# A fused scan and MLP kernel: block 0's preparation reordered, the first two scans put above the next block's preparation, and block 0's MLP input loaded from ScalarE's queue

## The chip, the cores and the metric

The kernel runs on one core of a Trainium2 chip. The metric is device time in microseconds (us), the median of three runs. Each core has a matrix engine (TensorE, PE in the profile), a vector engine (VectorE, DVE), an activation engine (ScalarE, ACT), GpSimd (POOL) and SyncE (SP), which in this kernel issues most of the DMAs. Each engine works through its own instructions strictly in the order in which the compiler wrote them, DMA issues included.

## The reference, cut to what matters

```python
# attention: 4 batches, 8 heads, 768 steps, head size 40
for t in range(S):
    y[:, :, t] = einsum('bhd,bhde->bhe', rt, state)
    Sa = einsum('bhde,bhe->bhd', state, at)
    state = state * wt - einsum('bhd,bhe->bhde', Sa, bt) + einsum('bhd,bhe->bhde', vt, kt)
x = y as (4*768, 320)
# MLP1, 320 -> 2048 -> 320
h = x @ w_in; g = maximum(h, 0) + alpha * minimum(h, 0); x = g @ w_out
# MLP2, 320 -> 1536 -> 320
g = x @ w_gate; out = (g * sigmoid(g) * (x @ w_val)) @ w_out
```

All arrays are fp32, except that weights reach the kernel as 64-bit words and are converted on the chip.

## The kernel before

The 768 time steps are cut into six blocks of 128. A block has four items, one for each batch; an item is one batch with 8 heads and 128 steps, and a scan goes through it in two chunks of 64 steps. Items are numbered 0 to 23, so items 0 to 3 are block 0.

**Preparation** (`prep_a`, `prep_b`, one pair for each item). ScalarE copies the decay into `wseg` (L540), VectorE scans it (L545, L552) and multiplies (`AN` L559 and `kbt`). TensorE makes `mnp` (L584) and the transposes `kbp` (L612). ScalarE takes the results out of PSUM: into `tt` (L590, L593), into `AN` (L597, which GpSimd then masks in L598) and into `KB` (L615). Four items fill one `tt`.

**Inverse** (`inverse(m)`, one for each block). It inverts the small triangular systems in `tt`: a VectorE transpose out of `tt` (L630), 31 steps on VectorE (L645, L653), two transposes (L656, L658), then TensorE's `eps` (L666) and `dps` (L685) with ScalarE copies between them. The second `eps` in the program is that of `inverse(1)`; no scan of block 1 can use its `tt` before that.

**Scan** (`seq(i, ch)`). One chunk runs around four engines: `zp` on TensorE (L749), `zs` on ScalarE (L751), `pp` on TensorE (L759), `ut` and `pv` on ScalarE (L761, L763), transposes on TensorE (L767, L771), `gs` and `s` on ScalarE (L773, L778), `gp` on TensorE (L782), a masked copy on VectorE, `yp` on TensorE (L797, L801), and the new state and `pv` on VectorE (L805, L809). After its second chunk a scan stores its output to `xd` in DRAM from ScalarE's queue (L817). The scan that comes next on the same side (`ch` is 0 or 1) begins with ScalarE's copy into `pv` (L717).

**MLP1** (`mlp1(j)`, one for each block). `fill_x` loads `xd[j]` into `xa` (L299, L303, four DMAs for a fill) and splits it into `xh`, `xl` (L218, L219) and `xst` (L304, L305). A step is 8 matmuls `u` (L274), the PReLU `g` (L314 on ScalarE, L315 on VectorE), the split into `gh` and `gl`, and 8 matmuls `d` (L280 to L286) of the step before. `mlp1(0)` is special: its first 8 steps run on the half of the columns that batches 0 and 1 give (256 wide), the next 8 on the other half, and only the rest on all 512. So the first half needs only scans 0 and 1.

**Weights** are converted in the first part of the program by all engines (`raw` to `wz`, `wy`, `wc`, `wd`).

MLP1 of the last blocks and all of MLP2 come after the last scan; MLP2 takes the last third of the time.

**What sets the order.** The generators above are interleaved by `drive(...)`, and each piece is given a priority by lowering or raising `tc.cur_priority`; a scheduler then writes out one order for each engine, a piece with a lower number first where its inputs allow. `lifted(n)` lowers the number by n inside it. Scans 0 and 1 run with `SP = 3000`, the preparation of block 1 (`rest1`, ending with `inverse(1)`) with `HP2 = 3000`, the fill of `mlp1` with `XPRI = 1000`.

Of the kernel before, what the change touches and what calls it, by code (L numbers as in the profile page):

```python
# [18 lines left out]
XPRI = 1000  # L19
# [44 lines left out]
L = 64  # L64
HALF = 32
LOOK = 2
TRB = 5
LATE = 20
XLEAD = 6
# [4 lines left out]
def kernel(  # L74
# [63 lines left out]
    def ago(n):  # L138
        return ups[-n] if len(ups) >= n else None
# [151 lines left out]
        xst = pool.tile([128, n], F32R, tag="xst", name="xst")  # L291
        return xh, xl, xst

    def fill_x(pool, xs, src, c0, c1):
        xh, xl, xst = (x[..., c0:c1] for x in xs)
        for j in range(3):
            xa = pool.tile([128, c1 - c0], F32, tag="xa", name="xa", bufs=XAB[0])
            if j < 2:
                nc.sync.dma_start(out=xa, in_=src[j * 128:j * 128 + 128])  # L299
                split(xa, xh[:, j], xl[:, j], nc.vector)  # L300
            else:
                for p in (lo, hi):
                    nc.sync.dma_start(out=xa[p], in_=src[256:DM])  # L303
                nc.scalar.copy(out=xst, in_=xa)  # L304
                nc.vector.tensor_tensor(out=xst[hi], in0=xa[hi], in1=xst[hi].bitcast(F32), op=ALU.subtract)  # L305

# [31 lines left out]
    def mlp1(j, early=0):  # L338
# [15 lines left out]
        seen = set()  # L354
        for f, c0, c1 in plan:
            if not seen & {(c0, c1), (0, half) if early and c0 == 0 else (c0, c1)}:
                with lifted(), held_by(ago(XLEAD) if j == NM - 1 else None):
                    b0, b1 = c0 // TB, c1 // TB
                    fill_x(xp1, xs, xd[j][:, b0:b1].rearrange("f b t -> f (b t)"), c0, c1)
                seen.add((c0, c1))  # L360
                yield
            t = fetch(wp1, 2 * f, True, j, done)
            ps = e1p["psu"].tile([128, c1 - c0], F32, tag="u", name="u")
            done.append(up_mm(ps, t, tuple(x[..., c0:c1] for x in xs)))
            yield
            if len(pend) == (2 if j == NM - 1 else DEP):
                down(*pend.pop(0))
            pend.append((f, c0, c1, *prelu(e1p["gp3"] if j == NM - 1 and fs.index(f) % 3 == 2 else gp1, ps, f, c1 - c0)))
            yield
# [196 lines left out]
    def prep_b(i):  # L566
# [14 lines left out]
        for g in range(2):  # L581
# [9 lines left out]
            for h, q in ((0, 1), (1, 3)):  # L591
                pr = slice(32 * q, 32 * q + 32)
                nc.scalar.copy(out=mc[pr, gsl, 0:HALF], in_=ps[pr, :, h, HALF:L])  # L593
            for h, pr in ((0, hi), (1, lo)):
                am = an[pr, h, g * SH:g * SH + SH]
                if AMK & (1 if i < B else 2 if i < 2 * B else 4):
# [5 lines left out]
                else:  # L602
                    mark["prep"] = nc.vector.tensor_tensor(
                        out=am, in0=ps[pr, :, h, :], in1=mask[pr].unsqueeze(1).to_broadcast([64, SH, L]), op=ALU.mult,
                    )
            yield
        kb = it["KB"] = (item_x if i < XI else item_q).tile([128, NSEG * 2 * D + 64 - D], F32, tag="KB", name="KB")
        nc.gpsimd.memset(kb[:, NSEG * 2 * D:], 0.0)
        for g in range(NSEG // 4):
            ps = bank([128, 4, 2, 64], "kbp", i)  # L610
            for j in range(4):
                nc.tensor.transpose(  # L612
                    ps[:, j].rearrange("p h e -> p (h e)"), kbt[:, 4 * g + j].rearrange("p j t -> p (j t)"), ident
                )
            nc.scalar.copy(  # L615
                out=kb[:, 8 * g * D:8 * (g + 1) * D].rearrange("p (s h e) -> p s h e", h=2, e=D), in_=ps[:, :, :, 0:D]
            )
            yield

    def scr(m, j):  # L620
# [269 lines left out]
        )  # L890
    else:
        drive(
            (seq(0, 0), N_SEQ, SP), (seq(1, 1), N_SEQ, SP),
            (take(rest1, int(nrest * RA)) if RA < 1 else rest1, FAC * nrest, HP2),
            (take(c1, NC1), NC1 - EC - EC0, CP),
        )
# [217 lines left out]
```

## Time and profile before

| what | value |
|---|---|
| median of three runs | 1230.73 us (1230.57, 1230.73, 1231.91) |
| profiled execution | 1229.82 us, its span 1228.1 us, granted clock 0.944 |
| PE busy | 1095.4 us, 89% of the span |
| DVE busy | 759.5 us, 62% |
| ACT busy | 602.0 us, 49% |
| POOL busy | 287.4 us, 23% |

The profiled execution is 0.91 us shorter than the median, and 1.7 us of it lie outside its span. Shares are means over stages that have different limits: the first 95 us hold the preparation and inverse of block 0, 95 to 220 us the first four scans with the preparation and inverse of block 1, 220 to 705 us the other scans beside MLP1, and what follows has no scan.

### The profile page before, as it was taken

What the parts mean: (1) busy time and instruction counts of PE and PEld (TensorE: products, weight loads), DVE (VectorE), ACT (ScalarE), POOL (GpSimd) and SP (SyncE); (2) the same over time, 40 slices, a digit from 0 to 9 for tenths busy, and PEclk for the clock granted to TensorE, in tenths of its full rate; (3) what the DMA queues carried; (4) which work ended last, traced back from release to release, by engine and by line L of the source; (5) the groups of instructions that cost most, each with busy time, mean ns of one, the idle gap of its engine ahead of it and who ended that gap; (6) DMA issues with size and microseconds to landing.
All of it is one profiled execution on the core that took longest, in us unless ns stands there. A gap on an engine that the chain in (4) does not pass through costs nothing. (4 is left out here: it accounts for less than half of the span.)

```text
span 1228.1 us, 24433 instructions
## 1 busy us (share of the span) xinstructions
PE 1095.4 (89%) x9056; PEld 934.2 (76%) x9056; DVE 759.5 (62%) x1624; ACT 602.0 (49%) x1495; POOL 287.4 (23%) x452
## 2 busy tenths in 40 slices
PE   4146687999999898899989999999999999999998
PEld 4145577877878787788777787787788888888887
DVE  7798988598589669949865434879522323223222
ACT  5559568655954665675655433545332323222222
POOL 8335433401212230341354000536300000000000
PEclk9669776988999998999999999999999999999999
DMA  5534688565554534645486464795010101010000
GB/s 146 186 133 147 214 271 288 172 193 171 158 156 135 175 114 145 194 153 154 125 280 210 148 206 138 250 353 164 1 48 1 48 1 48 1 37 13 22 1 22
DMA packets 94885, 166.36 MB, mean 135 GB/s; under 512 B 13232, under 2 KB 43184, under 8 KB 94768
## 3 DMA queue, kind: packets, MB, share of 16 engines
q1 hardware_dynamic: 86608, 160.88, 41.2%
q10 hardware_dynamic: 8160, 3.93, 1.1%
q8 instruction: 72, 1.18, 0.4%
q14 instruction: 45, 0.37, 0.1%
HBM read 136.98 MB, written 27.79 MB: 134 GB/s over the span
## 5 line engine op out<-in xcount | busy, mean ns | idle before, releaser
L218 ACT CAST gh<-g 128x512 fp32r<-128x512 f32 (+1 forms) x176 | 105.5, 600 | 162.8 <-DVE g L1050 116.2
L1050 DVE TENSOR_TENSOR g<-pv,sg 128x512 f32<-128x512 f32 x72 | 49.7, 691 | 206.3 <-PE pv L274 201.3
L219 DVE TENSOR_TENSOR gl<-g,gh 128x512 fp32r<-128x512 f32 (+1 forms) x176 | 121.9, 692 | 85.7 <-ACT gh L218 83.0
L274 PE MATMUL u<-xh,wt 128*128 128x512 f32 (+1 forms) x416 | 149.0, 401 | 13.5 <-DVE g L315 11.2
L315 DVE SCALAR_TENSOR_TENSOR g<-g,neg,u 128x512 f32<-128x512 f32 (+1 forms) x104 | 73.0, 703 | 88.9 <-ACT g L314 88.4
L274 PEld LDWEIGHTS u<-xh,wt 128*128 128x128 f32 x416 | 80.1, 196 | 32.7 <-DVE g L315 14.4
L314 ACT ACTIVATE g<-u 128x512 f32<-128x512 f32 (+1 forms) x104 | 58.6, 564 | 90.4 <-PE u L274 86.1
L274 PE MATMUL pg<-xh,w 128*128 128x512 f32 x288 | 102.6, 394 | 0.3 <-ACT sg L1048 0.3
L1048 ACT ACTIVATE sg<-pg 128x512 f32<-128x512 f32 x72 | 43.0, 598 | 120.6 <-PE pg L274 120.6
L274 PE MATMUL pv<-xh,w 128*128 128x512 f32 x288 | 100.5, 390 | 0.0
L1034 PE MATMUL o<-w,gh 128*128 128x320 f32 x288 | 87.5, 310 | 2.6 <-ACT gh L218 2.6
L1035 PE MATMUL o<-w,gh 128*128 128x320 f32 x288 | 87.8, 309 | 0.0
L281 PE MATMUL d<-gl,wt 128*128 128x512 f32 (+1 forms) x208 | 82.3, 398 | 1.2 <-DVE gl L219 1.2
L740 POOL COPY gs<-raw_v 64x160 f32<-64x160 f32 x96 | 40.8, 425 | 177.3 <-PE yp L797 108.6
L274 PE MATMUL u<-xl,wt 128*128 128x512 f32 (+1 forms) x208 | 80.8, 389 | 0.0
L653 DVE TENSOR_TENSOR la<-la,tmp 128x96 f32<-128x96 f32 (+43 forms) x306 | 79.3, 285 | 2.0
L282 PE MATMUL d<-gh,wt 128*128 128x512 f32 (+1 forms) x208 | 80.1, 387 | 0.0
L645 DVE TENSOR_TENSOR tmp<-la 128x96 f32<-128x96 f32 (+43 forms) x306 | 78.1, 279 | 1.8
L584 PE MATMUL mnp<-AN,kbt 128*128 128x128 f32 x384 | 59.6, 305 | 21.6 <-DVE AN L559 15.2
L598 POOL TENSOR_SCALAR_AFFINE_SELECT AN<-AN 64x256 f32<-64x256 f32 x96 | 52.2, 544 | 111.2 <-ACT AN L597 99.0
L1036 PE MATMUL o<-w,gl 128*128 128x320 f32 x288 | 77.2, 311 | 1.0 <-DVE gl L219 0.9
L280 PE MATMUL d<-gh,wt 128*128 128x512 f32 (+1 forms) x208 | 72.6, 402 | 2.8 <-DMA wt<-wd 2.8
(123 smaller groups left out, 2635.3 us busy)
## 6 DMA issues: line engine op xcount, KB each, us to landing
wt<-wd SPq DMA_DIRECT2D x98, 384.0 KB
wt<-wd SPq DMA_DIRECT2D x98, 320.0 KB
wd<-wc SPq DMA_DIRECT2D x24, 384.0 KB
raw<-in_moe_w_out_dram SPq DMA_DIRECT2D x28, 320.0 KB
raw_bk<-in_bk_dram SPq DMA_DIRECT2D x48, 160.0 KB
wd<-wc SPq DMA_DIRECT2D x20, 320.0 KB
raw<-in_moe_w_in_dram SPq DMA_DIRECT2D x16, 256.0 KB
raw_v<-in_v_dram SPq DMA_DIRECT2D x24, 160.0 KB
```

What stands on the lines that cost most here:

```text
L218: nc.scalar.copy(out=h, in_=raw)
L219: eng.tensor_tensor(out=l, in0=raw, in1=h.bitcast(F32), op=ALU.subtract)
L274: last = nc.tensor.matmul(ps, lt, rh, start=(i == 0), stop=(i == len(ops) - 1))
L280: nc.tensor.matmul(ps, wh, gh, start=first, stop=False)
L281: nc.tensor.matmul(ps, wh, gl, start=False, stop=False)
L282: nc.tensor.matmul(ps, wl, gh, start=False, stop=last)
L315: nc.vector.scalar_tensor_tensor(g, g, neg[:, f:f + 1], ps, ALU.mult, ALU.add)
L645: nc.vector.tensor_tensor(out=tv, in0=ml[:, kk + 1:HALF, kk:kk + 1].to_broadcast([128, nr, ns]), in1=tl[:, kk:kk + 1, c0:c0 + ns].to_broad ...
L653: mark["inv"] = nc.vector.tensor_tensor(out=dst, in0=dst, in1=tv, op=ALU.subtract)
L1034: nc.tensor.matmul(ops[q], gh[:, ts], wh, start=first, stop=False)
L1035: nc.tensor.matmul(ops[q], gh[:, ts], wl, start=False, stop=False)
L1036: nc.tensor.matmul(ops[q], gl[:, ts], wh, start=False, stop=last)
```

## The change

It has three parts.

1. `LATER = 800`: for the items of block 0, the copies into `AN` with their mask, and the whole `KB` part, get a number that is higher by 800, so that the `tt` copies of later groups may be put ahead of them.
2. `FIRST = 6000`: scans 0 and 1 run with 6000 in place of 3000, above the preparation of block 1.
3. The fill of `mlp1(0)` (both halves) is lifted by 6000 in place of 1000, and its `xa` DMAs are issued by ScalarE in place of SyncE.

```diff
-    def fill_x(pool, xs, src, c0, c1):
+    def fill_x(pool, xs, src, c0, c1, eng=nc.sync):
...
-                nc.sync.dma_start(out=xa, in_=src[j * 128:j * 128 + 128])
+                eng.dma_start(out=xa, in_=src[j * 128:j * 128 + 128])
...
-                    nc.sync.dma_start(out=xa[p], in_=src[256:DM])
+                    eng.dma_start(out=xa[p], in_=src[256:DM])
...
-                with lifted(), held_by(ago(XLEAD) if j == NM - 1 else None):
+                with lifted(XPRI if j else FIRST), held_by(ago(XLEAD) if j == NM - 1 else None):
...
-                    fill_x(xp1, xs, xd[j][:, b0:b1].rearrange("f b t -> f (b t)"), c0, c1)
+                    fill_x(xp1, xs, xd[j][:, b0:b1].rearrange("f b t -> f (b t)"), c0, c1, nc.sync if j else nc.scalar)
...
+            tc.cur_priority += LATER if i < B else 0
             for h, pr in ((0, hi), (1, lo)):
                 am = an[pr, h, g * SH:g * SH + SH]
...
+            tc.cur_priority -= LATER if i < B else 0
             yield
...
         for g in range(NSEG // 4):
+            tc.cur_priority += LATER if i < B else 0
             ps = bank([128, 4, 2, 64], "kbp", i)
...
+            tc.cur_priority -= LATER if i < B else 0
             yield
...
-            (seq(0, 0), N_SEQ, SP), (seq(1, 1), N_SEQ, SP),
+            (seq(0, 0), N_SEQ, FIRST), (seq(1, 1), N_SEQ, FIRST),
```

In the order that results, part 1 moves nothing: with it alone, the instructions of all five engines stand as before. Parts 2 and 3 move many. The lines of the changed kernel have numbers that are higher by 2 to 6.

First, TensorE in scans 0 and 1: `mnp` and `kbp` are the preparation of block 1, `ST_174` and `ST_176` the states of scans 0 and 1. Before:

```order
L584 MATMUL mnp<-AN,kbt 128x128 x4
L767 MATMUL pp<-ident,ut 128x128 x2
L771 MATMUL pp<-ident,ST_174 128x128 x2
L612 MATMUL kbp<-ident,kbt 128x128 x4
L584 MATMUL mnp<-AN,kbt 128x128 x4
L612 MATMUL kbp<-ident,kbt 128x128 x4
L767 MATMUL pp<-ident,ut 128x128 x2
L771 MATMUL pp<-ident,ST_176 128x128 x2
```

The same place in the changed kernel:

```order
L586 MATMUL mnp<-AN,kbt 128x128 x4
L773 MATMUL pp<-ident,ut 128x128 x2
L777 MATMUL pp<-ident,ST_174 128x128 x2
L617 MATMUL kbp<-ident,kbt 128x128 x4
L773 MATMUL pp<-ident,ut 128x128 x2
L777 MATMUL pp<-ident,ST_176 128x128 x2
L586 MATMUL mnp<-AN,kbt 128x128 x4
L617 MATMUL kbp<-ident,kbt 128x128 x4
```

Scan 1's transposes have moved ahead of one `mnp` and one `kbp` group of block 1.

Second, the first fill of `mlp1(0)`. In the kernel before it stood on SyncE's queue, among loads of inputs (`raw_vt`, `raw_a`, `raw_w`) and of weights (`raw`, `wd`):

```order
L527 DMA raw_vt_159<-in_vt_dram 40x512 x2
L492 DMA raw_a_142<-in_wa_dram 40x512 x2
L231 DMA raw<-in_moe_w_out_dram 128x640
L491 DMA raw_w_134<-in_wa_dram 40x512 x2
L527 DMA raw_vt_159<-in_vt_dram 40x512 x2
L299 DMA xa<-xd_57 128x256 x2
L244 DMA wd<-wc 128x640
```

In the changed kernel it stands on ScalarE, behind the store of scan 1 (`xd_57<-pv`) and ScalarE's work of scan 2, and its casts follow at once:

```order
L823 DMA xd_57<-pv 40x4x128 x2
L723 COPY pv<-raw_vt_159 128x2x2x64 x2
L757 COPY zs_168<-zp 64x4x40 x2
L767 COPY ut<-pp 128x256
L769 ACTIVATE pv<-pp 128x2x64 x2
L220 CAST wc<-wz 128x256
L220 CAST wc<-wz 128x64
L558 COPY Wx<-rest_114 128x8
L194 ACTIVATE wy<-raw 128x384
L542 COPY wseg<-raw_w_134 128x8x64
L301 DMA xa<-xd_57 128x256 x2
L305 DMA xa<-xd_57 64x256
```

The casts `xh<-xa` come one and three rows further on, the copy into `xst` twelve rows. On TensorE, 14 `u<-xst` matmuls (seven steps of MLP1, two each) stand ahead of `inverse(1)`'s `eps` before, and 16 (eight steps) now.

Third, TensorE in the second half of block 3, two scans side by side (`ST_178` and `ST_180`). Before, seven such rows followed each other with no row of MLP1:

```order
L749 MATMUL zp<-gs,AN 64x40 x16
L759 MATMUL pp<-tt_173,zs_164 64x64 x8
L759 MATMUL pp<-tt_173,zs_168 64x64 x8
L767 MATMUL pp<-ident,ut 128x128 x2
L771 MATMUL pp<-ident,ST_178 128x128 x2
L767 MATMUL pp<-ident,ut 128x128 x2
L771 MATMUL pp<-ident,ST_180 128x128 x2
```

In the changed kernel:

```order
L276 MATMUL u<-xst,wt 128x512 x2
L773 MATMUL pp<-ident,ut 128x128 x2
L777 MATMUL pp<-ident,ST_178 128x128 x2
L282 MATMUL d_5559<-gh,wt 128x512
L282 MATMUL d_5560<-gh,wt 128x512
L287 MATMUL d_5561<-gh,wt 128x512
L283 MATMUL d_5559<-gl,wt 128x512
L284 MATMUL d_5559<-gh,wt 128x512
L283 MATMUL d_5560<-gl,wt 128x512
L284 MATMUL d_5560<-gh,wt 128x512
L288 MATMUL d_5561<-gl,wt 128x512
L773 MATMUL pp<-ident,ut 128x128 x2
```

The eight `u` of a step now stand between `pp` and the first transposes, and eight `d` between the transposes of the two scans. TensorE's order differs up to the end of the last scan; from there on it is that of before, and as much of MLP1 is done by then.

## Rows read from the trace of the kernel before

**Rows 1.** The page's busy times, and the granted TensorE clock in 40 slices.

```profile
PE 1095.4 (89%) x9056; PEld 934.2 (76%) x9056; DVE 759.5 (62%) x1624; ACT 602.0 (49%) x1495; POOL 287.4 (23%) x452
...
PEclk9669776988999998999999999999999999999999
```

**Rows 2.** Busy time by stretch: PE, PEld, DVE, ACT, POOL, clock, DMA share, GB/s.

```profile
95.00:180.00 85.00, 62.45 (x651) 54.58 (x652) 75.70 (x201) 59.37 (x185) 39.82 (x63) 0.84 0.66 211
180.00:220.00 40.00, 30.52 (x449) 27.41 (x448) 34.08 (x58) 34.06 (x92) 17.02 (x25) 0.70 0.84 272
220.00:300.00 80.00, 75.82 (x936) 65.56 (x937) 62.22 (x182) 42.81 (x124) 16.92 (x40) 0.95 0.55 173
300.00:705.00 405.00, 381.44 (x4048) 318.53 (x4042) 293.76 (x700) 242.56 (x653) 110.76 (x194) 0.97 0.54 166
...
875.00:1228.00 353.00, 347.53 (x1799) 305.62 (x1797) 96.81 (x141) 92.99 (x164) 0.00 (x0) 1.00 0.06 21
```

**Rows 3.** Timeline, last item of block 0: start, duration, instruction, [idle before <-releaser].

```profile
38.26 0.76 ACT L597 COPY AN<-mnp 64x256 f32<-64x256 f32 x2
...
40.58 1.95 DVE L630 STREAM_TRANSPOSE la<-tt 128x1024 f32<-128x1024 f32 x1 [3.14 <-ACT tt L593]
```

**Rows 4.** Timeline of ScalarE (ACTq is its DMA issues), first fill.

```profile
131.35 1.20 ACTq L817 DMA_DIRECT2D xd<-pv  x2
133.79 0.71 ACT L717 COPY pv<-raw_vt 128x256 f32<-128x256 f32 x2 [2.49 <-DMA xd<-pv]
...
136.20 0.64 ACT L540 COPY wseg<-raw_w 128x512 f32<-128x512 f32 x1
...
143.88 0.69 ACT L218 CAST xh<-xa 128x256 fp32r<-128x256 f32 x2
...
149.18 0.40 ACT L304 CAST xst<-xa 128x256 fp32r<-128x256 f32 x1 [0.80 <-DMA xa<-xd]
```

**Rows 5.** Timeline of SyncE's DMA issues, first fill.

```profile
139.24 0.82 SPq L299 DMA_DIRECT2D xa<-xd  x2
...
145.52 1.23 SPq L303 DMA_DIRECT2D xa<-xd  x2
```

**Rows 6.** Timeline of TensorE, MLP1's first steps and the inverse of block 1.

```profile
150.09 0.50 PE L274 MATMUL u<-xst,wt 128*128 128x256 f32 x2 [1.99 <-DVE xst L305]
...
162.16 0.48 PE L280 MATMUL d<-gh,wt 128*128 128x256 f32 x2
...
163.08 0.28 PE L286 MATMUL d<-gl,wt 128*128 128x256 f32 x1
...
180.72 0.63 PE L274 MATMUL u<-xst,wt 128*128 128x256 f32 x2
186.34 3.62 PE L666 MATMUL eps<-la,tt 32*32 32x32 f32 x128 [4.99 <-DVE la L656]
```

**Rows 7.** Timeline of TensorE, waits inside later scans.

```profile
248.50 1.12 PE L759 MATMUL pp<-tt,zs 128*64 128x64 f32 x16 [2.40 <-ACT zs L751]
...
461.62 0.67 PE L749 MATMUL zp<-gs,AN 128*64 128x40 f32 x16 [1.51 <-DVE pv L809]
...
463.79 1.12 PE L759 MATMUL pp<-tt,zs 128*64 128x64 f32 x16 [0.81 <-ACT zs L751]
...
467.28 0.69 PE L767 MATMUL pp<-ident,ut 128*128 128x128 f32 x2 [1.31 <-ACT pv L763]
...
595.42 1.16 PE L782 MATMUL gp<-rbd,pv 128*128 128x128 f32 x8 [1.64 <-ACT s L778]
```

**Rows 8.** Busy time by stretch, around those waits of block 3.

```profile
460.00:470.00 10.00, 6.36 (x68) 5.34 (x65) 9.91 (x25) 7.86 (x27) 1.18 (x1) 0.65 0.67 193
470.00:480.00 10.00, 10.00 (x89) 7.90 (x87) 9.14 (x25) 2.69 (x5) 1.76 (x5) 0.83 0.38 114
```

**Rows 9.** The stores of `xd`: issues (ns min/median/max), and who waited for them.

```profile
L817 ACTq DMA_DIRECT2D xd<-pv x48: 280/300/1422, 129.2 to 704.7; - x48
...
  ACT pv L717: 23.2, 8
```

More of the change, by code (lines that the diff above doesn't have):

```diff
@@ L66 @@
 LOOK = 2
+FIRST = 6000
+LATER = 800
 TRB = 5
```

## The prediction

> **What bounds the kernel now.** I read the page first. TensorE is busy 89% of the span, the other engines far less [rows 1], so the kernel gains only where TensorE waits or runs at a low clock. The clock row shows where that is: low slices up to the seventh (which ends at 215 us), and once more an 8 in the sixteenth (460 to 491 us) [rows 1].
>
> The table by stretch says what each part is worth [rows 2]. From 95 to 180 us TensorE is busy 62.45 of 85 us, VectorE 75.70: VectorE is the tightest, with 9.3 us to spare, and ScalarE has 25.6. From 180 to 220 us TensorE has 30.52 of 40 at a clock of 0.70, VectorE and ScalarE 34 each. From 220 us on it changes: 75.82 of 80, then 381.44 of 405, then 347.53 of 353 in MLP2. There TensorE is the bound, and of MLP1's work whatever was done ahead of 220 us comes off the end at TensorE's own price. Between 300 and 705 us 23.6 us of idle are left in small waits, which a new order can find or lose.
>
> The chain in the front is that of `inverse(1)`. TensorE runs its seventh step of MLP1 up to 180.72 + 0.63 = 181.35 us and then waits 4.99 us for VectorE's transpose before `eps` [rows 6]. That wait is the one large place in the front where work could be put on TensorE for nothing.
>
> **The change, part by part.**
>
> *LATER.* The order with this line alone is that of before on every engine, so it costs and brings nothing. Had it moved the `AN` copies, the price would be small: VectorE's first transpose waits 3.14 us for `tt`, and a pair of `AN` copies ahead of the last `tt` copies takes 0.76 us [rows 3].
>
> *FIRST on scans 0 and 1.* It moves scan 1's transposes ahead of one `mnp` and one `kbp` group. VectorE has nearly the same work ahead of `inverse(1)`'s end as before (one split `gl` fewer), so I let `eps` start at 186.3 us as it did, and take nothing for this part by itself.
>
> *The fill from ScalarE.* In the trace scan 1's `xd` store is issued at 131.35 us, and ScalarE's next copy waits 2.49 us for it, until 133.79 [rows 4]. So the data is there at 133.8 us, but SyncE comes to the first `xa` load only at 139.24 and to the last at 145.52 [rows 5], with loads of inputs and weights ahead of it; `xh` is cast at 143.88 and `xst` at 149.18 [rows 4]. In the changed order ScalarE issues the loads behind `wseg`, which ran at 136.20 for 0.64 us; with the two `pv`, `wz` and `wy` pieces around it ScalarE comes there at about 137.5 us. Three issues ahead of the first cast take 0.3 us each by the median of ScalarE's other issues [rows 9]. The landing I take from the last `xa` pair: issued until 145.52 + 1.23 = 146.75, used at 149.18, 2.4 us. So `xh` is cast at about 137.5 + 1.0 + 2.4 = 140.9, which is 2.9 us earlier. The first step of MLP1 closed at 150.09 + 0.50 = 150.59 [rows 6]; it would close at 147.7. Six further steps took until 181.35, 5.1 us each; seven of them end the eighth at 147.7 + 35.9 = 183.6, which lies ahead of the `eps` at 186.34. That is what the changed order does too: eight steps stand ahead of `eps`, not seven.
>
> A step's `d` takes 163.08 + 0.28 - 162.16 = 1.20 us at full clock [rows 6], its `u` has as many matmuls of that size, so a step is 2.4 us of TensorE. *Term a:* this work leaves the part after 186 us, where it would be paid, and goes into the wait of 4.99 us: -2.4 us. Bounds 0 (the step moves only work that another engine paces) and -4.1 (the step at the low clock: the seventh's `u` began 2.1 us before 181.35, twice that).
>
> **Later places.** The order differs until 705 us, and I costed only tight places, where a scan's TensorE rows follow each other with under 1.2 us of other work.
>
> *Term b:* at 248.50 us `pp` waits 2.40 us for `zs` [rows 7]. About 1.2 us more of MLP1 now stands between `zp` and `pp` there: -1.2 us, bounds 0 and -2.4.
>
> *Term c:* in block 3 three waits follow each other: 1.51, 0.81 and 1.31 us [rows 7]. The changed order puts a step's `u` and `d` between `pp` and the second transposes, which covers the last: -1.3 us, bounds 0 and -3.6 (all three). The clock there is 0.65 and then 0.83 [rows 8], part of it at the lower of its two levels (1.2 GHz), after a stretch with TensorE busy 6.36 of 10. Full clock would be worth at most 10 x 0.35 + 10 x 0.17 = 5.2 us. Nothing says how much of it the better cover keeps; I choose a fifth: -1.0 us, bounds 0 and -5.2.
>
> *Term d:* `gp` at 595.42 waits 1.64 us [rows 7]. Most of the `eps` of the inverse of block 5 now stand between those transposes and `gp`, and a whole set of 128 took 3.62 us [rows 6], so this wait is covered: -1.6, bounds 0 and -1.6.
>
> *Term e:* eight issues more on ScalarE, 2.4 us by the median [rows 9], nearly all inside its 25.6 idle us; but casts stand right behind the loads, so ScalarE may sit through two landings of 2.4 us with scan 2's copies queued behind them, and TensorE and VectorE behind those. I take +0.5; bounds 0 and +4.8.
>
> *Term f:* waits newly laid bare. Scans 2 and 3 stand later against MLP1 than before, and in block 5 one `zp` to `pp` place loses 1.4 us of cover. +1.0, bounds 0 and +3.6 (as much as the three waits of term c).
>
> Sum: -2.4 - 1.2 - 1.3 - 1.0 - 1.6 + 0.5 + 1.0 = -6.0. On the profiled execution 1229.82 - 6.0 = 1223.8; the median of before stands 0.9 above that execution, so **1224.7 us**.
>
> **The rivals.**
>
> *ScalarE stalls (slower).* ScalarE issues in order. If it comes to the loads before scan 1's store has landed, or to the casts before `xa` has, it waits with scan 2's copies behind it. For it: it already waited 2.49 us for a store at this very place, such waits come to 23.2 us over eight scans [rows 9], and VectorE, which takes its work from the scans, has only 9.3 us to spare ahead of 180 us. Two landings of 2.4 us, and the low clock (0.70) kept for 5 us longer behind them, push `inverse(1)` by about 5 us: about 1235. Against it: five other pieces stand between the store's wait and the loads. It decides when ScalarE's waits from 133 to 150 us grow by more than the 2.7 us by which `eps` had room (186.34 - 183.6).
>
> *Nothing comes of it.* VectorE's work ahead of `inverse(1)` is the same but for a `gl`; from 180 to 220 us ScalarE is busy 34.06 of 40, so a step less there only makes TensorE wait for ScalarE instead, and the later places cancel: about 1230.3.
>
> *The loads come no earlier, the later waits still shrink.* If the first load is late because of the transfers beside it and not because of SyncE's place in its queue, term a is 0 and part of b to d stays: about 1227.5. The DMA engines are 0.66 busy in this stretch [rows 2], which speaks for it; that SyncE issued 5.4 us after the store had landed speaks against it [rows 4, 5]. The Trainium skill, DMA: Bandwidth & Descriptors, section "Issuing engines are not separate DMA queues", says that DMAs from ScalarE, SyncE or GpSimd run on the same 16 engines, and that another issuer only saves the sequencer's time to start them, usually small beside the transfer. By that rule this rival is the likelier; the trace agrees with it as to the transfer (2.4 us against 0.3 for an issue), but the wait in the queue ahead is 5.4 us, of which the rule says nothing.
>
> *The later order loses.* The same scheduler that covers the waits of b to d may lay bare others in 400 us that I didn't cost: with term a kept and the waits of 300 to 705 us growing by a fourth of their 23.6 us, +5.9, the time is 1230.73 - 2.4 + 5.9 = 1234.2.
>
> **How the numbers follow.** A difference of 0.2%, 2.5 us, is about what a measurement of this kernel can tell from none. Chances: the forecast 0.45; loads no earlier 0.22; nothing 0.07; ScalarE's stall 0.14; the later order 0.12. The forecast's own range is 1219.5 to 1228.5: a, b and c at their far bounds (5.2 us more), or half of the 7.5 us of gains. For 8 in 10 I go from 1216, where most of the full clock in block 3 is added to the former, to 1235.5, which takes in both slower rivals. Faster takes the forecast and half of the second, 0.56; within 0.2% the other half and the case of nothing, 0.18; slower the last two, 0.26.
>
> **What would show it.** Right: the first `xa` issue at 137 to 138 us on ScalarE, `xh` cast near 141, eight steps of MLP1 and a wait under 3 us ahead of an `eps` at 186 us, TensorE busy more than 65 us of 95 to 180, and no clock of 0.65 at 460 us. Wrong: ScalarE idle for over 3 us at an `xh` cast; `eps` later than 188 us; the front the same and the gain or loss all between 220 and 705 us. What I trust least is the later order: its waits were costed at five places, and one lost stretch of full clock weighs as much as term a.

## The result and the profile after

The changed kernel took 1241.49 us (median of four runs, 1238.68 to 1243.66) against 1230.86 us before: a ratio of 1.0084 with a 95% interval of 1.0062 to 1.0105. It is slower by 0.84%, and 1241.49 lies outside the range of 1216 to 1235.5.

The page of the changed kernel, its busy times and the granted clock in 40 slices, beside [rows 1]:

```profile
PE 1094.5 (88%) x9056; PEld 930.0 (75%) x9056; DVE 759.5 (61%) x1624; ACT 603.6 (49%) x1495; POOL 288.2 (23%) x452
...
PEclk9667797999999898999989999999999999999999
```

The span went from 1228.1 to 1236.9 us. TensorE is busy as long as before (1094.5 and 1095.4), so the 8.8 us are idle time: 1236.9 - 1094.5 = 142.4 us against 132.7. The stretches of [rows 2] say where:

```profile
95.00:180.00 85.00, 63.49 (x656) 54.94 (x656) 78.95 (x211) 60.28 (x186) 36.98 (x65) 0.80 0.68 217
180.00:220.00 40.00, 31.07 (x472) 27.77 (x469) 32.66 (x52) 32.88 (x88) 16.26 (x23) 0.79 0.80 260
220.00:300.00 80.00, 74.68 (x931) 64.60 (x932) 65.39 (x184) 44.48 (x128) 18.32 (x40) 1.00 0.59 184
300.00:705.00 405.00, 375.67 (x3956) 310.55 (x3950) 286.60 (x688) 239.61 (x645) 113.33 (x194) 0.96 0.53 161
```

From 95 to 220 us TensorE does 1.6 us more, at a lower clock up to 180 us (0.80 for 0.84) and a higher one behind it (0.79 for 0.70). From 300 to 705 us its idle grows from 23.6 to 29.3 us. To see where the time goes, the busy time times the granted clock is summed over windows of 10 us. By this sum the changed kernel is 3.5 us ahead of before at 200 us, 2.7 ahead at 300, 0.6 behind at 320, 3.6 behind at 420 and 6.3 behind at 680. One trace gives such a sum only to a few us. At 200 us seven traces of the runs further on that still have the order of before lie from 3.6 us behind to 0.8 ahead, and four that have the changed order 1.9 to 5.1 ahead: there is a lead, but its size is not sure.

The front did much of what was forecast. ScalarE's timeline at the first fill, which answers to [rows 4, 5], with the store of scan 1 on its first row:

```profile
134.32 0.70 ACTq L823 DMA_DIRECT2D xd<-pv  x2
...
139.17 0.86 ACTq L301 DMA_DIRECT2D xa<-xd  x2
140.07 1.57 ACTq L305 DMA_DIRECT2D xa<-xd  x1
142.35 0.41 ACT L220 CAST xh<-xa 128x256 fp32r<-128x256 f32 x1 [3.22 <-DMA xa<-xd]
...
143.52 0.41 ACT L220 CAST xh<-xa 128x256 fp32r<-128x256 f32 x1 [0.77 <-DMA xa<-xd]
143.84 0.71 ACT L723 COPY pv<-raw_vt 128x256 f32<-128x256 f32 x2
144.45 0.36 ACT L767 COPY ut<-pp 128x256 f32<-128x256 f32 x1
...
147.10 0.40 ACT L306 CAST xst<-xa 128x256 fp32r<-128x256 f32 x1
```

and TensorE's timeline, with scan 3's `pp`, the first step's first and last matmuls, the eighth step's, and `eps`, which answers to [rows 6]:

```profile
136.93 1.12 PE L765 MATMUL pp<-tt,zs 128*64 128x64 f32 x16 [0.73 <-ACT zs L757]
...
142.81 0.58 PE L276 MATMUL u<-xh,wt 128*128 128x256 f32 x1 [3.71 <-ACT xh L220]
...
149.36 0.48 PE L276 MATMUL u<-xst,wt 128*128 128x256 f32 x2
...
183.44 0.40 PE L276 MATMUL u<-xst,wt 128*128 128x256 f32 x2
183.77 2.21 PE L672 MATMUL eps<-la,tt 32*32 32x32 f32 x128
```

`xh` is cast 1.5 us earlier than before. ScalarE does no other work for 3.22 + 0.77 us at the two casts; the issuing of DMAs is not counted as busy, and 0.86 + 1.57 us of it are the issues of the first three loads, so that about 1.5 us are left as waiting for data. Scan 3's `pp` ends at 138.05 us, but ScalarE copies it (`ut`) only at 144.45, behind the issues and the casts. TensorE waits 3.71 us for `xh`. The eighth step ends at 183.84 us, and `eps` starts 2.6 us earlier with no wait left: the wait of 4.99 us is gone. TensorE's longest waits from 220 us to the last scan are these (one window each):

```profile
255.12 0.39 PE L282 MATMUL d<-gh,wt 128*128 128x256 f32 x1 [2.58 <-DMA wt<-wd]
305.67 1.16 PE L586 MATMUL mnp<-AN,kbt 128*128 128x128 f32 x8 [1.76 <-ACT tt L699]
312.51 1.22 PE L282 MATMUL d<-gh,wt 128*128 128x512 f32 x2 [3.27 <-ACT gh L220]
...
627.00 0.76 PE L276 MATMUL u<-xh,wt 128*128 128x512 f32 x1 [2.97 <-DMA wt<-wd]
...
673.42 0.69 PE L765 MATMUL pp<-tt,zs 128*64 128x64 f32 x16 [2.14 <-ACT zs L757]
```

None of the five stands among the waits of [rows 7]. The one at 312.51 comes back, with 3.2 to 3.4 us, in all three traces of other runs that have the changed order there. It is followed back on ScalarE's timeline and on VectorE's:

```profile
303.07 0.71 ACT L723 COPY pv<-raw_vt 128x256 f32<-128x256 f32 x2 [2.61 <-DMA raw_vt<-in_vt_dram]
...
308.53 0.60 ACT L316 ACTIVATE g<-u 128x512 f32<-128x512 f32 x1
311.22 0.20 ACT L558 COPY Wx<-rest 128x8 f32<-128x8 f32 x1 [2.09 <-DVE Wx L554]
311.33 0.61 ACT L542 COPY wseg<-raw_w 128x512 f32<-128x512 f32 x1
311.85 0.61 ACT L220 CAST gh<-g 128x512 fp32r<-128x512 f32 x1
```

```profile
309.89 1.24 DVE L554 TENSOR_TENSOR_SCAN Wx<-wseg,first 128x520 f32<-128x520 f32 x1
311.05 0.72 DVE L317 SCALAR_TENSOR_TENSOR g<-g,neg,u 128x512 f32<-128x512 f32 x1
```

ScalarE's part of the step's `g` stands behind a `pv` copy that waits 2.61 us for its input. It is done at 309.13 us, but VectorE's part (L317) stands behind the scan into `Wx` and ends at 311.77; the cast into `gh`, which needs both, follows at 311.85. ScalarE's own wait of 2.09 us is for the same scan and costs `gh` next to nothing. So the orders of ScalarE and of VectorE make the wait: the `pv` copy and the `Wx` scan have nothing to do with this step of MLP1.

### The profile page after: what moved, and what is told of

Its sections match the earlier page's. It is cut to its first block, busy times and chain, and to the rows that moved or that the text cites. A ratio compares the mean times of both kernels' runs of the same rounds, so it can differ in the third digit from the quotient of the medians.

```text
span 1236.9 us, 24420 instructions
## 1 busy us (share of the span) xinstructions
PE 1094.5 (88%) x9056; PEld 930.0 (75%) x9056; DVE 759.5 (61%) x1624; ACT 603.6 (49%) x1495; POOL 288.2 (23%) x452
## 4 chain that ended last, share of the span: by engine, by line
PE 56%; DVE 17%; DMA 10%; ACT 10%; issue 4%; SPq 2%; POOL 0%; ACTq 0%; DVEq 0%; POOLq 0%
PE pv L276 10%; PE pg L276 10%; PE u L276 9%; PE o L1042 3%; PE o L1041 3%; PE o L1040 3%; DMA xd<-pv 3%; DVE tmp L651 2%; DVE la L659 2%; PE d L282 2%; PE d L283 2%; DMA wt<-wd 2%; PE d L284 2%; PE gp L788 2%; PE yp L803 2%
## 5 line engine op out<-in xcount | busy, mean ns | idle before, releaser
L317 DVE SCALAR_TENSOR_TENSOR g<-g,neg,u 128x512 f32<-128x512 f32 (+1 forms) x104 | 72.8, 701 | 85.0 <-ACT g L316 84.7
L746 POOL COPY gs<-raw_v 64x160 f32<-64x160 f32 x96 | 43.5, 453 | 151.4 <-PE yp L803 54.5
L586 PEld LDWEIGHTS mnp<-AN,kbt 128*128 128x128 f32 x384 | 53.1, 215 | 32.3 <-DVE AN L561 13.6
```

What stands on the lines that cost most here:

```text
L586: nc.tensor.matmul(ps[:, s].rearrange("p h t -> p (h t)"), kbt[:, g * SH + s].rearrange("p j t -> p (j t)"), an[:, :, g * SH + s, :],)
```

## The experiments

Three theories were set against each other. *Stall:* ScalarE sits at the fill's loads and casts, scans 2 and 3 come late, and the scan chain carries that on. *Later order:* the scheduler writes another order for all that follows, and that order has worse waits. *Cover runs out:* MLP1's first block is done earlier, so TensorE has nothing to put beside the scans at the border of two blocks. All ratios are to the kernel before on the same chip, five rounds each. The ratios and their 95% intervals come from all runs and are not quotients of the medians given, from which they differ by about 0.1% at most.

### Parts of the change alone

Scans 0 and 1 first, nothing else (`LATER` is 0 in all four):

```diff
-            (seq(0, 0), N_SEQ, SP), (seq(1, 1), N_SEQ, SP),
+            (seq(0, 0), N_SEQ, FIRST), (seq(1, 1), N_SEQ, FIRST),
```

> Only scans 0 and 1 rank above the preparation of block 1; the fill of the first MLP block stays on SyncE's queue at its old priority. Theory 'stall' (ScalarE sits at the loads and casts of the fill, scans 2 and 3 come 5 to 7 us late and the scan chain never gets that back): no such loads here, so scans 2 and 3 are within 2 us of before and the time is 1229 to 1232 us. Theory 'later order' (the loss is made by the order that the scheduler writes past 220 us, which every edit to the front re-rolls): the front changes by under 2 us but the sum of TensorE's waits from 220 to 705 us moves by several us either way, so the time is off 1230.9 by more than 2.5 us in one direction or the other, and the shift is found in those waits. Theory 'cover runs out' (the first MLP block is done earlier by some 12 us, so that TensorE has nothing to put beside the scans at the border of two blocks): no earlier fill, so no loss, 1229 to 1232 us.

Measured: 1249.32 us, 1.0157 (1.0133 to 1.0180).

The fill lifted and issued by ScalarE, scans as before:

```diff
-                with lifted(), held_by(ago(XLEAD) if j == NM - 1 else None):
+                with lifted(XPRI if j else FIRST), held_by(ago(XLEAD) if j == NM - 1 else None):
...
-                    fill_x(xp1, xs, xd[j][:, b0:b1].rearrange("f b t -> f (b t)"), c0, c1)
+                    fill_x(xp1, xs, xd[j][:, b0:b1].rearrange("f b t -> f (b t)"), c0, c1, nc.sync if j else nc.scalar)
```

> Only the fill of the first MLP block is lifted and issued by ScalarE; scans 0 and 1 keep their priority. Theory 'stall': scans 2 and 3 late by 5 us or more as in the changed kernel, 1238 to 1243 us. Theory 'later order': again another order past 220 us, so anything from 1225 to 1243 us, with the shift in the waits from 220 to 705 us; the delay of scans 2 and 3 does not tell the time. Theory 'cover runs out': an eighth step ahead of the inverse of block 1 and the first MLP block done about 12 us earlier, with a wait of 3 us at about 310 us: 1238 to 1243 us.

Measured: 1231.22 us, 0.9995 (0.9976 to 1.0014).

The same lift, loads left on SyncE:

```diff
-                with lifted(), held_by(ago(XLEAD) if j == NM - 1 else None):
+                with lifted(XPRI if j else FIRST), held_by(ago(XLEAD) if j == NM - 1 else None):
```

> The fill is lifted in priority but its loads stay on SyncE's queue; scans as before. Theory 'stall': nothing waits on ScalarE for its own loads, so 1228 to 1232 us. Theory 'later order': off by some us either way, in the waits past 220 us, whatever the front does. Theory 'cover runs out': if the first steps come as early as in the changed kernel, 1238 us or more, else 1230 us.

Measured: 1227.54 us, 0.9963 (0.9946 to 0.9980): this one beats both kernels.

Both priorities, loads on SyncE (the first and the third diff together):

> The whole change but for the queue: scans 0 and 1 first, the fill lifted, its loads on SyncE. Theory 'stall': 1228 to 1232 us, with scans 2 and 3 earlier by 4 us or more than in the changed kernel. Theory 'later order': its own place between 1225 and 1243 us, not the sum of the effects of the parts. Theory 'cover runs out': between 1236 and 1243 us if the first MLP block is done as early as in the changed kernel (about 302 us).

Measured: 1227.64 us, 0.9965 (0.9947 to 0.9983).

What follows: the parts don't add up. Scans first costs 1.57% alone and nothing beside the lifted fill (0.9965 for 0.9963). Two pairs differ in the queue of the loads: with the fill lifted, ScalarE in place of SyncE gives 0.9995 for 0.9963, and with scans first as well 1.0084 for 0.9965 (the two kernels of this second pair differ in `LATER` too, which alone moves nothing). So without the move to ScalarE's queue the change would have gained a third of a per cent. Nor did the fill need that queue to come early. With the lift alone SyncE issues the first load at 137.14 us, and the first step of MLP1 closes 4.7 us earlier than in the changed kernel:

```profile
137.14 0.80 SPq L301 DMA_DIRECT2D xa<-xd  x2
...
140.26 0.44 ACT L220 CAST xh<-xa 128x256 fp32r<-128x256 f32 x1
...
144.66 0.50 PE L276 MATMUL u<-xst,wt 128*128 128x256 f32 x2
```

The stall theory loses ground: the slowest of the four has no load of the fill on ScalarE's queue, and the fill alone on ScalarE gives 0.9995, though scans 2 and 3 are only 2.4 us late there (the next section has the stronger test). "Cover runs out" falls: it asked for 1238 us or more with the fill alone, whose first block of MLP1 is stored 6 us earlier than before, as in the changed kernel, and nothing is lost. The later order asked for a shift and got three in four; but two of its ranges were so wide (1225 to 1243 us) that this is weak support. Nor does the front tell the time: by the same sum of busy time and clock TensorE was, at 200 us, 1.6 us behind (scans first), 4.1 ahead (fill only), 0.5 ahead (fill lifted), 3.2 behind (both on SyncE), and the times go in no such order; but traces of one order differ by as much. The longest wait of scans first is at one row of TensorE, and on ScalarE stands what holds it:

```profile
515.42 2.07 PE L586 MATMUL mnp<-AN,kbt 128*128 128x128 f32 x8 [7.68 <-ACT tt L699]
```

```profile
510.19 0.21 ACT L558 COPY Wx<-rest 128x8 f32<-128x8 f32 x1 [3.01 <-DVE Wx L554]
...
512.95 0.71 ACT L723 COPY pv<-raw_vt 128x256 f32<-128x256 f32 x2 [1.62 <-DMA xd<-pv]
...
514.18 2.40 ACT L699 ACTIVATE tt<-dps 32x512 f32<-32x512 f32 x4
```

ScalarE's `tt` copies stand behind a copy that waits for VectorE and one that waits for a store. TensorE's next row waits for these copies, and its next row of MLP1 stands at 520.56 us. The same wait of 7.68 us is found at 521.51 us in the first run of the next section, which has this order only past 400 us.

### One order up to a seam, the other behind it

Here the order is written out by hand. A list names every instruction, and each is tied to the one ahead of it on its engine, with no semaphore:

```diff
+        if e in last:
+            tc.add_manual_dep(
+                x, last[e], mybir.DependencyInfo(mybir.DependencyClass.NoSync, mybir.DependencyReason.DATA), reason="order",
+            )
+        last[e] = n
...
         tile_rwkv_moe_kernel(tc, *args)
+        in_order(tc)
```

The first four lists have their seam later than their expectations say: at the last `dps` of the inverse of block 3, about 400 us, and not of block 1. The numbers expected hold for either; what they tell apart is the order up to 400 us from the order past it.

```diff
-order: before
+order: before up to the seam, scans_first_only behind it
```

> The program is that of before, and the order is written out by hand for all five engines: up to the last dps of the inverse of block 1 (about 200 us) as in the kernel before, behind it as in the run where only scans 0 and 1 were put first (1249.3 us). Theory 'later order' (the time is made by the order past 200 us): 1244 to 1250 us. Theory 'front' (the loss starts with the late scans 0 to 3 ahead of 200 us and is carried on): 1229 to 1233 us.

Measured: 1252.33 us, 1.0176 (1.0145 to 1.0206).

```diff
-order: before
+order: scans_first_only up to the seam, before behind it
```

> The reverse: up to the last dps of the inverse of block 1 the order of the run with scans 0 and 1 put first, behind it that of the kernel before. Theory 'later order': 1229 to 1235 us. Theory 'front': 1244 to 1250 us. If both this and the run with the parts exchanged are slow, it is the seam between a front and an order that was made for another front.

Measured: 1233.32 us, 1.0022 (0.9998 to 1.0047).

```diff
-order: changed
+order: changed up to the seam, before behind it
```

> The changed kernel (loads of the first fill on ScalarE, all of its priorities) with its own order up to the last dps of the inverse of block 1, and behind it the order of the kernel before. Theory 'later order': the 3.5 us that TensorE's work was ahead at 200 us are kept, 1226 to 1230 us. Theory 'front': 1238 to 1243 us. Theory 'cover runs out': the eighth step is still done early and the first MLP block ends earlier, 1234 us or more, with a wait of 3 us near 310 us.

Measured: 1231.42 us, 1.0001 (0.9978 to 1.0025).

```diff
-order: before
+order: before up to the seam, changed behind it
```

> The program of before with its own order up to the last dps of the inverse of block 1, and behind it the order of the changed kernel. Theory 'later order': 1241 to 1246 us, the loss without the gain. Theory 'front': 1229 to 1233 us.

Measured: 1240.76 us, 1.0081 (1.0055 to 1.0107).

Each of the four lies within 2.4 us of what "later order" gave and far from what "front" gave. This settles the place. The changed order past 400 us costs 0.81% though the front is that of before, and the changed front, with its ScalarE loads, late scans and early eighth step, costs and brings nothing that shows (1.0001) when the old order follows. With it the stall falls. Scans first behaves alike: 1.76% past the seam, 0.22% ahead of it. The next runs move the seam.

```diff
-order: changed
+order: changed up to inverse(1)'s last dps, before behind it
```

> The four runs with exchanged parts had their seam later than their expectations say: it lay at the last dps of the inverse of block 3 (about 400 us), not of block 1. So they put the loss of the change past 400 us and say that its order up to 400 us is worth nothing. This run has the seam at the last dps of the inverse of block 1 (about 200 us): the changed kernel's order ahead of it, that of the kernel before behind it. Theory 'gain kept' (TensorE's total decides, so the 3.5 us that its work was ahead at 200 us stay, and the changed order of 200 to 400 us ate them): 1226 to 1228.5 us. Theory 'cover runs out' (the first MLP block just ends earlier, while the second can't begin before the last scan of block 1 is stored, so that the lead is lost at about 310 us whatever order follows): 1229.5 to 1232 us, with some 3 us of waits more than before between 300 and 320 us.

Measured: 1234.22 us, 1.0034 (1.0012 to 1.0055). It doesn't tell the theories apart: the old order does not fit the new front, and TensorE waited 6.16 us at the seam itself, for `tt` ahead of an `mnp` at 203.49 us.

```diff
-order: before
+order: before up to inverse(4)'s last dps, changed behind it
```

> The order of before up to the last dps of the inverse of block 4 (about 510 us), that of the changed kernel behind it. With the seam at 400 us the loss was 10 us. If the places at 408 to 415 us (waits of 1.6, 1.7 and 1.4 us) make the most of it: 1232 to 1235 us. If the places past 610 us (a wait of 2.97 us for weights at 627 us, one of 2.14 us at 673 us, each followed by a low clock) make the most: 1237 to 1241 us.

Measured: 1233.12 us, 1.0029 (1.0004 to 1.0055).

```diff
-order: before
+order: before up to inverse(5)'s last dps, changed behind it
```

> The same with the seam at the last dps of the inverse of block 5 (about 609 us). If the loss is made past 610 us: 1236 to 1241 us. If it is spread evenly over 400 to 705 us: 1233 to 1235 us. If it is made before: 1230 to 1232 us.

Measured: 1237.70 us, 1.0060 (1.0038 to 1.0082).

```diff
-order: changed
+order: changed up to inverse(5)'s last dps, before behind it
```

> The reverse: the changed kernel's order up to the last dps of the inverse of block 5, that of before behind it. If the loss is made past 610 us: 1230 to 1234 us. If it is made between 400 and 610 us: 1237 to 1241 us. Together with the run that exchanges the two parts it tells whether the parts add up to 10 us, or whether each order fits only its own beginning (both slow).

Measured: 1234.93 us, 1.0043 (1.0017 to 1.0068).

```diff
-order: changed
+order: changed up to inverse(2)'s last dps, before behind it
```

> The changed kernel's order up to the last dps of the inverse of block 2 (about 300 us), that of before behind it. In the changed kernel TensorE's work was ahead by some 3 us at 300 us and no longer at 320, where it waits 1.76 us for tt and 3.27 us for gh. Theory 'the order of 300 to 320 us eats it': with the order of before there the lead stays, 1226 to 1228.5 us and under 2 us of waits between 300 and 320. Theory 'the lead is not worth anything' (ScalarE's queue and the scans set the pace there, whatever the order): 1229 to 1232 us, with the waits of that stretch 3 us longer than before.

Measured: 1229.01 us, 1.0000 (0.9978 to 1.0021). It too has a wait at its seam (6.09 us), so the lead is lost there and whether another order could keep it stays open.

Of the 0.84%, about 0.4 are made from 400 to 610 us and about 0.6 past 610 us; the two sum to a little more than the whole, within their intervals. The run with the seam at 510 us doesn't fit: 0.29 where at least 0.6 was to be had behind it (its interval reaches 0.55). By its own expectation it puts most of the loss at the waits of 408 to 415 us.

The traces bear on both places. From the last `dps` of the inverse of block 5 to the last `yp` of the last scan, the four traces with the changed order past 610 us take 99.5 to 100.9 us, and the six with the order of before 90.6 to 94.3. The means differ by 7.8 us, 0.6%. And between 400 and 420 us the three traces that have the changed order from the start up to 610 us at least fall behind by 3.9 to 5.9 us, by busy time times clock, while nine with the order of before there move by -1.6 to +2.9. But the run whose changed order begins at 400 us shows no such drop, so that place is pointed at and not shown.

### By which engine

Past 610 us the two orders were mixed by engine: everything as before, but SyncE's issues as in the changed kernel; and the reverse.

```diff
-order: before
+order: before, but SyncE past inverse(5)'s last dps as changed
```

> The order of before everywhere, but past the last dps of the inverse of block 5 (about 609 us) SyncE's DMA issues stand in the changed kernel's order. If the 0.6 per cent that the order past 610 us costs come from when SyncE issues the weight loads (the wait of 3 to 4 us at 627 us for a weight tile): 1235 to 1239 us. If they come from the order on the computing engines: 1229 to 1232 us.

Measured: 1237.63 us, 1.0068 (1.0047 to 1.0090).

```diff
-order: before
+order: before, but all engines save SyncE past inverse(5)'s last dps as changed
```

> The exchange: past 610 us TensorE, VectorE, ScalarE and GpSimd in the changed kernel's order, SyncE in that of before. If SyncE's order makes the loss: 1229 to 1232 us and under 2.5 us of wait for weights at 627 us. If the computing engines' order makes it: 1235 to 1239 us, with the wait of 2 us for zs at 673 us.

Measured: 1232.45 us, 1.0023 (1.0003 to 1.0043). The time is what "SyncE's order" asked for, but not the wait for weights, which was to stay under 2.5 us:

```profile
623.47 0.70 PE L419 MATMUL d<-gh,wt 128*128 128x512 f32 x2 [3.56 <-DMA wt<-wd]
```

So in the kernel before it is enough to change the order in which SyncE issues some DMAs. From the inverse of block 5 to the last `yp` the trace with SyncE's order takes 97.4 us, the one with the other engines' 95.1. The first of these two runs, SyncE's timeline and one row of TensorE:

```profile
612.47 0.70 SPq L666 DMA_DIRECT2D raw_vt<-in_vt_dram  x2
616.14 0.35 SPq L383 DMA_DIRECT2D wd<-wc  x1
616.58 0.38 SPq L403 DMA_DIRECT2D wt<-wd  x1
619.13 0.38 SPq L365 DMA_DIRECT2D raw<-in_moe_w_gate_dram  x1
...
620.13 1.01 SPq L438 DMA_DIRECT2D xa<-xd  x2
...
623.97 1.01 SPq L403 DMA_DIRECT2D wt<-wd  x2
```

```profile
629.31 0.76 PE L413 MATMUL u<-xh,wt 128*128 128x512 f32 x1 [3.91 <-DMA wt<-wd]
```

The kernel before has there:

```profile
608.83 0.70 SPq L527 DMA_DIRECT2D raw_vt<-in_vt_dram  x2
611.82 0.83 SPq L299 DMA_DIRECT2D xa<-xd  x2
...
614.77 0.82 SPq L264 DMA_DIRECT2D wt<-wd  x2
615.70 0.37 SPq L244 DMA_DIRECT2D wd<-wc  x1
...
617.37 0.71 SPq L264 DMA_DIRECT2D wt<-wd  x1
```

A store of a converted weight (`wd<-wc`) and a load into a staging buffer (`raw`) have moved ahead of the fill and the weight loads. Neither is ready: SyncE issues nothing from 613.2 to 616.1 us (2.9 us of it until GpSimd is done with `wc`) and from 617.0 to 619.1 (2.1 us until ScalarE's `wz` frees the buffer), and the pair of `wt` loads goes out 11.5 us behind `raw_vt` instead of 5.9. TensorE waits 3.91 us for weights. Its longest wait for them there in the kernel before:

```profile
620.48 1.19 PE L280 MATMUL d<-gh,wt 128*128 128x512 f32 x2 [2.37 <-DMA wt<-wd]
```

That wait grows by 1.5 us, the time by 0.68%, some 8 us, and the exchange has nearly the same wait at a third of the loss. So that SyncE's order costs time is shown; that it does so through this wait is not.

Three rows alone, in the kernel before:

```diff
 DMA raw_vt_159<-in_vt_dram 40x512 x2
+DMA wd<-wc 128x768
+DMA raw<-in_moe_w_gate_dram 128x2x256
+DMA raw<-in_moe_w_gate_dram 64x256
 DMA xa<-xd_61 128x512 x2
...
 DMA wt<-wd 128x768
-DMA wd<-wc 128x768
-DMA raw<-in_moe_w_gate_dram 128x2x256
-DMA raw<-in_moe_w_gate_dram 64x256
 DMA wt<-wd 128x640
```

> The kernel before, every engine in its own order, but for three rows of SyncE at about 612 us: one store of a converted weight (wd) and two loads of raw gate weights stand ahead of the fill of the fifth MLP block (xa) and of the two weight loads (wt) behind it, as they do in the changed kernel. If SyncE's queue, held up by a store whose data isn't ready, is what costs the 0.6 to 0.7 per cent of the part past 610 us: 1234 to 1239 us, SyncE's weight loads some 5 us later than before and a wait of 3 to 4 us for weights near 627 us. If it is the other, small exchanges of that order behind 630 us: 1229 to 1232 us.

Measured: 1236.37 us, 1.0038 (1.0013 to 1.0062), with this wait for weights:

```profile
624.63 1.19 PE L421 MATMUL d<-gh,wt 128*128 128x512 f32 x2 [3.38 <-DMA wt<-wd]
```

Three of SyncE's 759 DMA issues make the kernel slower, by more than half of what SyncE's whole order past 610 us does.

The opposite, in the changed kernel:

```diff
-order: changed
+order: changed, with fifteen rows of SyncE at 612 us as in before
```

> The changed kernel with its own order on every engine, but for those fifteen rows of SyncE at about 612 us (xa, raw_vt, wt, wd and raw), which stand in the order of the kernel before. If they are the cause, some 0.5 per cent come back: 1233 to 1236 us, without the wait of 3 us for weights at 627 us. If not: 1239 to 1243 us.

Measured: 1239.76 us, 1.0066 (1.0042 to 1.0089): a miss. The changed kernel stays slow, and a wait for weights is there by another way:

```profile
610.99 0.66 SPq L671 DMA_DIRECT2D raw_vt<-in_vt_dram  x2
615.13 0.83 SPq L443 DMA_DIRECT2D xa<-xd  x2
```

```profile
623.78 0.70 PE L424 MATMUL d<-gh,wt 128*128 128x512 f32 x2 [4.06 <-DMA wt<-wd]
```

Now SyncE stands still from 611.7 to 615.1 us at the fill `xa`, which waits for a scan's store, with the weight loads behind it again. Against the 1.0084 of the whole change 0.18% came back, and by the two intervals it may be anything from nothing to half a per cent, so what these rows cost in the changed kernel stays open. They don't cost it in the same way: in the changed kernel itself the `wd` store goes out 0.1 us behind `raw_vt` and holds nothing up. The two orders have to be taken as wholes.

### An edit in the other direction

```diff
-HP2 = 3000
+HP2 = 3200
```

> Not a part of the change: the kernel before with the preparation of block 1 at 3200 in place of 3000, the opposite of what the change does to scans 0 and 1. The front should move by under 4 us. Theory 'later order' (any edit in the front makes the scheduler write another order for 700 us, good or bad by several us): off 1230 us by more than 2.5 us in one direction or the other, with the shift past 200 us. Theory 'scans first is what hurts': the opposite edit gains or does nothing, 1222 to 1231 us.

Measured: 1241.33 us, 1.0088 (1.0058 to 1.0117). Raising the preparation of block 1 above the scans costs as much as the change, which set two scans above that preparation. That speaks against "scans first is what hurts". But the front moved far more than the 4 us that were expected, so the run does not tell the front from the later order: the first step of MLP1 closes 10.7 us later, four steps and not seven stand ahead of `eps`, and the longest wait of the trace is in the front. Past 290 us the longest is one of 5.17 us, for VectorE at 629.45.

```profile
185.82 0.55 PE L280 MATMUL d<-gh,wt 128*128 128x256 f32 x1 [9.46 <-DMA wt<-wd]
```

## Why the prediction was wrong

*The front: right in kind, half in size.* Eight steps stand ahead of `eps`, the 4.99 us wait is filled, and the eighth step ends at 183.84 us (forecast 183.6). The loads went out at 139.17 us and not at 137.5: scan 1's store, which stands ahead of them on ScalarE, came at 134.32 us and not at 131.35 [rows 4]. The prediction took "nothing for this part by itself" for putting scans 0 and 1 first; but in the nine traces that do so this store is issued at 133.7 to 135.5 us, and in the ten that have scans and preparation as before at 130.3 to 133.1. From the first issue to the cast it took 3.2 us (forecast 1.0 + 2.4). So `xh` came 1.5 us earlier and not 2.9, and the first step 0.75 us; the steps then ran every 4.9 us in place of 5.1. `eps` itself came 2.6 us earlier, which was not forecast.

*The stall: it happened, and did not decide.* The first chunks of scans 2 and 3 ended 5 to 6 us later than before, of which scans 0 and 1 brought about 2. Term e was priced too low: the eight issues took ScalarE 4.9 us, from 0.35 to 1.57 us each, and not 2.4. (The 2.49 us by which a `pv` copy waited [rows 4] likewise hold 1.20 us of issuing.) `inverse(1)` was not pushed, and the run with this front and the old order past 400 us gives 1.0001.

*Term a: the first step that failed* is "whatever was done ahead of 220 us comes off the end at TensorE's own price". The lead that was there at 200 us is gone by 320: between 300 and 320 us each of the four traces with the changed order loses 2.9 to 3.7 us of it, while seven with the order of before move by 0.6 at most. In the changed kernel that is 1.76 + 3.27 us of waits at 305 and 312 us, where the kernel before has none of over 0.5 us. That TensorE is busy 95% of a stretch does not make it the bound at each place of it. (The clock row has an 8 also in its ninth and tenth slices, 246 to 307 us, which the reading of [rows 1] left out.) Terms a, b and e, all ahead of 400 us, come to -3.1 us; the run with the changed order up to there has +0.1 (-2.7 to +3.1). That the order and not a lack of MLP1 work makes those waits is read from the timelines of ScalarE and VectorE; the runs meant to show it lost the lead at their seams.

*The later places: the step that set the sign.* Terms c, d and f, all past 400 us, come to -2.9 us; the run with the changed order from there on has +0.81%, 10 us (6.8 to 13.2). On the trace, at 249 us 2.40 became 0.63 + 0.93, but 2.58 us for weights followed at 255 (b); in block 3 3.63 us became 1.25 + 0.68 + 1.39 + 0.67 = 3.99, and the clock 0.79 and 0.87 in place of 0.65 and 0.83 (c); at 595 us 1.64 became 1.06 ahead of `eps` and 0.35 (d). These come to little. Term f, waits newly laid bare, was mis-sized: +1.0 us, where the loss past 400 us is 10. Most of the part past 610 us goes through SyncE's queue, where no place was costed at all. Only TensorE's own rows were compared, and only for cover.

*The rivals.* "The later order loses" is what happened; it had 0.12 and a price of +3.5 us on the median, where 10.6 were measured. "The loads come no earlier" held in so far as the queue was not what was needed: the lift alone brought SyncE to the first load at 137.14 us, the time forecast for ScalarE. The rule of the Trainium skill, DMA: Bandwidth & Descriptors, section "Issuing engines are not separate DMA queues", weighs only the time to start a DMA. By it the choice of the queue should hardly matter. With the fill lifted it made 0.3%, and with scans first as well 1.2%; and as the changed front alone gives 1.0001, the loss came through the order behind it. What stands behind a DMA in its engine's own order is not in the rule, and past 610 us that was 0.4 to 0.7%.

*What stays open:* which places from 400 to 610 us make up the 0.4%, how SyncE's order past 610 us costs more than the wait for weights grows, and whether any order keeps the lead of 200 us.

## What to carry to other kernels

Where a scheduler orders five queues from priorities, an edit of the first 200 us is also a new order for the next 500, and that can outweigh the edit: here six edits of the front gave from -0.4 to +1.6%. So compare the orders of all engines to the end, and ask at each DMA queue what stands behind a transfer that isn't ready; or fix the rest of the order by hand and change one part. Change the priority and the queue of a transfer in separate runs: here the priority alone brought the fill early. To find the place of a loss, splice the two orders at a seam and move it, and look at the seam's own wait before reading the result; then time a whole stretch between two instructions, as a single wait can mislead.

## What the hardware showed that was not expected

The kernel before was first seen in three runs within 0.11%, but 29 runs of it beside the first four experiments spread from 1226.97 to 1238.04 us, and 28 beside the next four from 1219.68 to 1236.46. The profiled execution of one kernel can thus differ from its median by as much as the effect sought, also in parts where two programs are the same: a difference of a few us is read from ratios over many runs, and single waits only where the same wait comes back in several traces, as the one at 312 us does.

One DMA that is not ready holds a queue. SyncE's issues stood still for 2.9 us at one store and for 2.2 at one load, with loads behind them. The Trainium skill, PSUM — Partial Sum Buffer, section "Engine vs sequencer instructions", calls the queues of ScalarE, VectorE and GpSimd strict FIFOs. The traces agree for ScalarE: scan 3's `pp` was done at 138.05 us, and its copy, behind the issues and casts of the fill, ran at 144.45.
